# Reordering SyncE's transfers and the last unit's output in a hand-scheduled attention and MLP kernel

## The chip, the cores and the metric

The kernel runs on one core of one Trainium2 chip, as one program in one launch. The metric is the device time of that launch in microseconds (us); less is better. The core has five engines that run side by side and wait for each other through semaphores: TensorE (PE, matrix multiplies), VectorE (DVE), ScalarE (ACT, exponentials and copies), GpSimd (POOL) and SyncE (SP), which here does nothing but issue transfers (DMAs). Each engine executes its own queue strictly in order, so an instruction that waits holds up everything behind it on its engine.

## The reference

All tensors are float32; S is 2048, D is 512, there are 32 heads of 16, and F is 1792.

```python
def _A_ref(x, wqkv, wo):                       # attention
    qkv = (x @ wqkv).reshape(B, S, 3, H, Dh)...
    scores = einsum("bhqd,bhkd->bhqk", q, k) * Dh ** -0.5
    o = einsum("bhqk,bhkd->bhqd", softmax(scores), v)
    return o.transpose(...).reshape(B, S, D) @ wo

def _B_ref(x, w1, b1, w2, b2):                 # MLP
    h = maximum(x @ w1 + b1, 0) ** 2
    return h @ w2 + b2

xn = _layernorm(x)
return x + _A_ref(xn, A_wqkv, A_wo) * _silu(_B_ref(xn, B_w1, B_b1, B_w2, B_b2))
```

## The kernel before

**Units and slots.** The attention is cut into 32 units: unit `u` is four heads (`u // 4`) and 512 query positions (`u % 4`). A unit is worked through in 16 steps of 128 keys, so there are 512 steps, and step `st` is done in a *slot* with the number `st`. A slot holds the four score products of a step (`exp_mm`, one PE product and one exponential on ACT for each head), the product of the exponentials with V two steps back (`pv_step(st - 2)`, PE line L401, into the one bank `po`), row maxima of a unit 24 steps ahead (`max_mm`, DVE line L324), and a piece of dense work (MLP or output projection), which an iterator hands out. PE's order is written by hand; the other four engines get their instructions in the order in which the Python code emits them. `later(n, fn)` emits `fn` at the start of the slot `n` later than now.

**The tail.** From slot 486 on no row maxima are left, and the order of a slot is a plain one of exponentials and the last output projections: `wo_last(c)` takes tiles `k = 16 + 4c + tt` of 128 rows, two slots each. For each tile PE makes three products in two halves into the one bank `pd_t` (L223), DVE multiplies the bank with the gate `g` (L759) and adds the partial sum `s` (L760), and SP stores the rows (L761). The next tile may use the bank only after L759. The operands of tiles 16 to 19 come from one load `oc` (`wo_load(0, [3])`), those of tiles 20 to 23 from another (`wo_load(1, [3])`, L677), which reads what the normalised units 28 and 29 stored in `on_d`. Tiles 24 to 27 use unit 30 directly, and tiles 28 to 31 are done at the very end.

**Three chains that cross SP's queue.**
- *Unit 29's normalisation* (`evac`): after its last `pv_step` the bank is copied (ACT), the sums are gathered (SP, L419), inverted (DVE, L425), stored to `r_d` (SP, L428), loaded back broadcast over the partitions into `hl` (SP, `evac_back`, L433), multiplied and split into a high and a low part (POOL, L439 to L441), and stored to `on_d` (SP, four transfers, L448). Only then can `oc` for tiles 20 to 23 be loaded. `EVAC_LAST` gives the slots, counted from the evacuation, at which these steps are emitted.
- *Unit 31's shift* (`shift`): the row maxima of a unit are transposed, negated and split (DVE, L368 to L371), stored to `sh_d` (SP, L377), and loaded as rows into `qe` (SP, four transfers, L392), where the score products read them. Slot 496 is the first that needs unit 31's.
- *The loads of `g` and `s`* (`wo_ask`, L704 and L710), two tiles ahead, and the load of `q6` (L777), which is read at the end.

**The end** (`unit_final`): after the last `pv_step`, DVE transposes each half of `po` in blocks of 32 (`unit_turn`, L789), inverts the sums that stand in one row of each block (L795), multiplies (L796) and transposes back (L799); ACT makes the high part of `thl` (L849), DVE the low part (L854). PE has meanwhile put twelve products of unit 30's neighbours into four banks (L808) and adds three products for each of the four tiles (L861). Then come a gate (`gate`, DVE, L868) and an addition (L872) for each tile, the first two additions on POOL with their stores on ACT's queue, the last two on DVE with stores on SP.

Of the kernel before, what the change touches and what calls it, by code (L numbers as in the profile page):

```python
# [9 lines left out]
F32 = mybir.dt.float32  # L10
F32R = mybir.dt.float32r
AF = mybir.ActivationFunctionType
ALU = mybir.AluOpType
# [4 lines left out]
P = 128  # L18
S = 2048
D = 512  # L20
H = 32
DH = 16
# [5 lines left out]
NU = NQ * 4  # L28
# [4 lines left out]
NPT = 17  # L33
NVT = 7
EVAC = (1, 6, 7, 9, 11, 14)
EVAC_LAST = (1, 3, 4, 5, 7, 9)
GAPS = (24,)
FIRST = 2
W1_LOADS = (13, 14, 16, 20, 23)
# [15 lines left out]
def kernel(  # L55
# [11 lines left out]
    nc = tc.nc  # L67
    xf = x.rearrange("b s d -> (b s) d")
    of = out.rearrange("b s d -> (b s) d")
# [42 lines left out]
    with ExitStack() as ph:  # L112
# [81 lines left out]
        late = []  # L194
# [4 lines left out]
        def later(n, fn):  # L199
            if n:  # L200
                waiting.append((now[0] + n, fn))
            else:
                fn()
# [124 lines left out]
        def max_end(g):  # L328
            for u in [u for u, n in left.items() if n == 0]:
                del left[u]  # L330
                m4 = m4s[u % 2]
                nc.vector.tensor_reduce(m4[:, :16], mxs[u], axis=AX.X, op=ALU.max)
                mxs[u] = m4
                late.append((g + (8 if u == 3 else 6 if u else 0), u))
            u, s = divmod(g, 16)
            if u >= NU:
                return
            qd, qc = divmod(u, 4)
            if qd == 0:
                if qc == 2 and s % 2 == 0 and s < 12:  # L340
                    load_k(1, s // 2)
                if qc == 3 and 9 <= s < 15:
                    load_k(1, s - 3)
            else:
                if qc == 2 and qd + 1 < NQ and s % 2 == 0:
                    load_k(qd + 1, s // 2)
                if qc == 3 and qd + 1 < NQ and s % 2 == 0 and s < 8:
                    load_k(qd + 1, 8 + s // 2)
            if u == 3 and s == 8:
                for j in range(2):  # L350
                    rows = slice(64 * j + 3 * DH, 64 * j + 4 * DH)
                    nc.sync.dma_start(
                        rot["ka"][3][rows, :].bitcast(F32), rot["ka"][2][rows, :].bitcast(F32)
                    )
            at = (12, 14) if u == 1 else (8, 9)
            if s in at:
                load_q_pair(u, "qe", at.index(s), qes.setdefault(u, []))
            at = (6, 10) if u == 1 else (7, 11)
            if s in at and u + 1 < NU:
                load_q_pair(u + 1, "qm", at.index(s), qms.setdefault(u + 1, []))  # L360
# [5 lines left out]
        def shift(u):  # L366
            tr = sp.tile([P, 32], F32, name="tr", bufs=1)
            nc.vector.transpose(tr, mxs[u])  # L368
            sh = sp.tile([P, 2, 32], F32R, name="sh", bufs=1)
            nc.vector.tensor_scalar(sh[:, 0], tr, -1.0, None, op0=ALU.mult)  # L370
            nc.vector.scalar_tensor_tensor(  # L371
                sh[:, 1], tr, -1.0, sh[:, 0].bitcast(F32),
                op0=ALU.mult, op1=ALU.subtract,
            )

            def keep():
                nc.sync.dma_start(  # L377
                    sh_d[u].rearrange("b c i n -> (b c) i n"), sh.bitcast(F32)
                )

            def back():
                for p in range(2):
                    for i in range(2):
                        shift_rows(u, p, i)

            later(1, keep)
            later(2 if u else 6, back)

        to_block = []

# [234 lines left out]
        tail = {}  # L625
# [118 lines left out]
        def wo_last(c):  # L744
            for tt in range(4):
                k = 16 + 4 * c + tt
                wo_ask(k + 2)
                if k in GAPS:
                    yield None, None
                if c == 2 and tt == 3:  # L750
                    [wo_ask(30), wo_ask(31)]
                if k == 18:
                    wo_load(1, [3])
                t0 = c * 512 + tt * P
                g, s = wos.pop(k)
                ps = pd.tile([P, D], F32, name="pd_t")

                def post():
                    nc.vector.tensor_tensor(g, ps, g, op=ALU.mult)  # L759
                    nc.vector.tensor_tensor(g, g, s, op=ALU.add)  # L760
                    later(2, lambda g=g, t0=t0: nc.sync.dma_start(of[t0 : t0 + P, :], g))  # L761

                done_d[0] = ps
                if c < 2:
                    terms = wo_terms(ps, wos["l", c], tt, [3])
                else:
                    hl, w, ts_ = tail["hl"], tail["w67"], slice(tt * P, (tt + 1) * P)
                    terms = terms3(ps, [(
                        lambda a, q, hl=hl, ts_=ts_: hl[q, a, ts_], lambda b, q, w=w: w[q, b]
                    )])  # L770
                yield from halves(terms, (3,), post, 1)
# [21 lines left out]
        def unit_back(i, rows, sm):  # L793
# [5 lines left out]
            nc.vector.transpose(ot, rows.rearrange("p b r -> p (b r)"))  # L799
            return ot  # L800

        def unit_q6(pss, c, tts):

            def both(a, b, n):
                for h, (ps, tt) in enumerate(zip(pss, tts)):
                    r = slice(64 * h, 64 * h + 64)
                    w = tail["w6"][r, b] if h else wos["w"][r, b, 3]
                    nc.tensor.matmul(  # L808
                        ps, wos["q", c][r, a, tt * P : (tt + 1) * P], w, start=(n == 0), stop=False
                    )  # L810

            return [
                lambda n=n, a=a, b=b: both(a, b, n)
                for n, (a, b) in enumerate(((0, 0), (0, 1), (1, 0)))
            ]
# [23 lines left out]
        def unit_final(po):  # L839
            pss = [pm.tile([P, 512], F32, name="pm_t") for tt in range(3)]  # L840
            pss.append(pd.tile([P, 512], F32, name="pd_t"))
            for step in unit_q6(pss[:2], 3, (0, 1)) + unit_q6(pss[2:], 3, (2, 3)):
                step()
            parts = [wos.pop(28 + tt) for tt in range(4)]
            hls, ots = [], []
            for i in range(2):
                ot = unit_back(i, *unit_turn(po, i))
                hl = tail["p"].tile([P, 2, 256], F32R, name=f"thl{i}")
                nc.scalar.activation(hl[:, 0], ot, AF.Copy)  # L849
                hls.append(hl)  # L850
                ots.append(ot)

            def low(i):
                nc.vector.tensor_tensor(  # L854
                    hls[i][:, 1], ots[i], hls[i][:, 0].bitcast(F32), op=ALU.subtract
                )

            def out(tt, n):
                a, b = ((0, 0), (0, 1), (1, 0))[n]
                t = tt % 2  # L860
                nc.tensor.matmul(  # L861
                    pss[tt], hls[tt // 2][:, a, t * P : (t + 1) * P], tail["w7"][:, b],
                    start=False, stop=(n == 2),
                )

            def gate(tt):
                g = parts[tt][0]
                nc.vector.tensor_tensor(g, pss[tt], g, op=ALU.mult)  # L868

            def add(tt, a, b, eng, queue):  # L870
                g, s = parts[tt]
                eng.tensor_tensor(g[:, a:b], g[:, a:b], s[:, a:b], op=ALU.add)  # L872
                queue.dma_start(of[1536 + tt * P : 1536 + (tt + 1) * P, a:b], g[:, a:b])

            low(0)
            for tt, n in ((0, 0), (0, 1), (1, 0), (1, 1), (0, 2), (1, 2)):
                out(tt, n)
            low(1)
            for tt in (2, 3):
                for n in range(3):  # L880
                    out(tt, n)
            gate(0)
            add(0, 0, D, nc.gpsimd, nc.scalar)
            gate(1)
            add(1, 0, D, nc.gpsimd, nc.scalar)
            gate(2)
            gate(3)
            add(2, 0, D, nc.vector, nc.sync)
            add(3, 0, D, nc.vector, nc.sync)

        ph.enter_context(tc.manual_schedule(engines={mybir.EngineType.PE}))
        qs = ExitStack()
# [520 lines left out]
        def dense():  # L1413
            mp = ExitStack()
            yield from mlp_tasks(mp)
            mp.close()
            early.close()
            wo_pools()
            wo_load(0, [0, 1, 2])
            wo_ask(0)  # L1420
            wo_ask(1)
            for _ in range(2):
                yield [], None
            later(3, wo_small)
            yield from wo_part()
            for c in range(3):
                if c == 0:
                    o3.close()
                    wos["q6"] = right(wstk, "q6p", 1)
                    later(3, lambda: load_q6(3))  # L1430
                yield from wo_last(c)

        odd = itertools.chain((0,) * 4, itertools.cycle((1, 0)))
# [178 lines left out]
```

## Time and profile before

| | us |
|---|---|
| three runs | 1628.72, 1630.25, 1631.37 (median 1630.25) |
| profiled execution, its own time | 1627.99 |
| its span, first to last instruction | 1626.2 |
| PE, DVE, ACT, POOL busy | 1610.3, 1362.1, 1188.9, 520.5 |

The profile is of one execution. Its span is 1.8 us shorter than its own time, and that time is 2.26 us below the median of the three runs. Times in the traces count from the start of the span. A busy PE is not a PE at its peak, because matrix products overlap. The granted clock of PE was 0.999 over the span. `SPq` and `ACTq` rows are transfers being issued: the time in such a row is the issuing, not the transfer. In the timeline a number in brackets behind a row is the idle time before it with what ended it.

### The profile page before, as it was taken

How to read it: one execution, taken by the hardware profiler on the slowest of the kernel's cores; microseconds unless marked ns; L12 is line 12 of the kernel's file. 1: busy time of each engine (PE TensorE's matmuls, PEld its weight loads, DVE VectorE, ACT ScalarE, POOL GpSimd, SP SyncE). 2: the span in 40 equal slices, each digit the busy share in tenths (PEclk: the TensorE clock that was granted, in tenths of full speed). 3: DMA queues.
4: the chain of work that ended last, by engine and by line, in shares of the span. 5: the costliest groups of instructions: out<-in, count | busy, mean ns of one | idle time of the engine just before them, and what ended most of it. 6: DMA issues, size and time to landing. Idle time of an engine off the chain costs nothing.

```text
span 1626.2 us, 36026 instructions
## 1 busy us (share of the span) xinstructions
PE 1610.3 (99%) x13656; PEld 936.1 (58%) x13656; DVE 1362.1 (84%) x2359; ACT 1188.9 (73%) x2349; POOL 520.5 (32%) x547
## 2 busy tenths in 40 slices
PE   8999999999999999999999999999999999999998
PEld 6899665556545654664466456545654565445543
DVE  6486888888888888888888888888888888887744
ACT  7212777777777777877777777777777777777786
POOL 6436667133113310321133112311331133226421
PEclk9999999999999999999999999999999999999999
DMA  8877556434343333434343334423542252247564
GB/s 297 235 236 233 175 162 157 127 96 128 81 103 96 103 88 90 127 87 110 83 119 93 85 87 130 112 68 83 141 112 67 70 155 78 55 126 210 188 179 150
DMA packets 163565, 208.16 MB, mean 128 GB/s; under 512 B 59168, under 2 KB 79136, under 8 KB 161824
## 3 DMA queue, kind: packets, MB, share of 16 engines
q1 hardware_dynamic: 163104, 205.33, 44.6%
q8 instruction: 108, 1.77, 0.5%
q14 instruction: 65, 0.53, 0.1%
q10 hardware_dynamic: 288, 0.52, 0.1%
HBM read 148.64 MB, written 55.56 MB: 126 GB/s over the span
## 4 chain that ended last, share of the span: by engine, by line
PE 98%; DVE 1%; DMA 0%; issue 0%; SPq 0%; DVEq 0%; ACT 0%; ACTq 0%
PE po L401 31%; PE pd_t L255 20%; PE pm_t L317 16%; PE se L1201 14%; PE pd_t L223 7%; PE pm_t L1077 4%; PE pd_t L1077 1%; PE se L1047 1%; PE se L981 1%; PE se L317 1%; PE pm_t L1163 0%; PE pd_t L1047 0%; DVE mx L324 0%; DMA xt<-in_A_x_dram 0%; PE pm_t L1201 0%; PE po L981 0%
## 5 line engine op out<-in xcount | busy, mean ns | idle before, releaser
L324 DVE TENSOR_REDUCE mx<-pm_t 128x1 f32<-128x512 f32 x1927 | 1197.3, 684 | 166.9 <-PE pm_t L317 74.0
L1213 ACT ACTIVATE pt<-se 128x512 f32<-128x512 f32 x1996 | 1035.5, 614 | 252.8 <-PE se L1201 210.4
L317 PE MATMUL pm_t<-ka,qm 64*128 64x512 f32 x1927 | 769.6, 420 | 0.0
L1201 PE MATMUL se<-qe,ka 64*128 64x512 f32 x1996 | 673.0, 396 | 0.3 <-ACT pt L1213 0.3
L401 PE MATMUL po<-pt,v 128*32 128x512 f32 x4096 | 545.3, 604 | 0.2 <-DVE tsm L795 0.2
L317 PEld LDWEIGHTS pm_t<-ka,qm 64*128 64x128 f32 x1927 | 338.3, 184 | 237.0 <-DVE mx L324 225.5
L1201 PEld LDWEIGHTS se<-qe,ka 64*128 64x128 f32 x1996 | 337.2, 184 | 18.1 <-ACT pt L1213 1.7
L255 PEld LDWEIGHTS pd_t<-xc,w1s 64*128 64x128 f32 x2352 | 292.0, 186 | 82.2 <-issue 82.2
L255 PE MATMUL pd_t<-xc,w1s 64*128 64x256 f32 x2352 | 332.2, 288 | 0.0
L255 PE MATMUL pd_t<-w2t,hT 64*128 64x512 f32 x1080 | 300.6, 410 | 0.0
L255 PEld LDWEIGHTS pd_t<-w2t,hT 64*128 64x128 f32 x1080 | 179.0, 184 | 83.2 <-issue 75.5
L555 POOL TENSOR_TENSOR r<-r 128x512 f32<-128x512 f32 x56 | 58.2, 1039 | 370.3 <-ACT r L552 370.3
L401 PEld LDWEIGHTS po<-pt,v 128*32 128x32 f32 x4096 | 81.0, 108 | 159.9 <-issue 136.8
L574 POOL TENSOR_TENSOR u<-u,b_t 128x512 f32<-128x512 f32 x16 | 20.6, 1289 | 320.2 <-ACT u L573 286.3
L324 DVE TENSOR_REDUCE mx<-se 128x1 f32<-128x512 f32 x121 | 77.9, 686 | 26.0 <-PE se L317 26.0
L439 POOL TENSOR_TENSOR ot<-ot,hl 128x512 f32<-128x512 f32 x30 | 38.6, 1286 | 173.9 <-DMA hl<-r_d 132.7
L223 PE MATMUL pd_t<-wot,oc 64*128 64x512 f32 x336 | 90.2, 405 | 0.4 <-issue 0.3
L552 ACT ACTIVATE r<-pd_t,b_t 128x256 f32<-128x256 f32 x112 | 47.0, 470 | 57.0 <-PE pd_t L255 53.8
L223 PEld LDWEIGHTS pd_t<-wot,oc 64*128 64x128 f32 x336 | 58.4, 184 | 46.9 <-ACT pt L1213 12.6
L1077 PE MATMUL pm_t<-xT,wr_t 64*128 64x512 f32 x408 | 73.8, 388 | 0.0
L97 POOL TENSOR_TENSOR hT<-r,hT 128x512 fp32r<-128x512 f32 x56 | 72.3, 1291 | 4.7
L223 PE MATMUL pd_t<-w2t,hT 64*128 64x512 f32 x264 | 68.8, 393 | 0.0
(134 smaller groups left out, 1148.4 us busy)
## 6 DMA issues: line engine op xcount, KB each, us to landing
w1s<-w_d SPq DMA_DIRECT2D x196, 256.0 KB
qm<-q_d SPq DMA_DIRECT2D x384, 32.0 KB
ka<-k_d SPq DMA_DIRECT2D x96, 128.0 KB
qe<-q_d SPq DMA_DIRECT2D x384, 32.0 KB
q_d<-hl SPq DMA_DIRECT2D x16, 512.0 KB
g<-g_d SPq DMA_DIRECT2D x32, 256.0 KB
k_d<-hl SPq DMA_DIRECT2D x15, 512.0 KB
hl<-r_d SPq DMA_DIRECT2D x30, 256.0 KB
```

The source lines that it names most:

```text
L97: (lo or nc.gpsimd).tensor_tensor(dst[1], raw, dst[0].bitcast(F32), op=ALU.subtract)
L223: mm = nc.tensor.matmul(out_, lh(r), rh(r), start=first_ and lane == 0, stop=last_ and lane == 1, skip_group_check=True,)
L255: mm = nc.tensor.matmul(out_, lh(r), rh(r), start=first_ and lane == 0, stop=last_ and lane == 1, skip_group_check=True,)
L317: nc.tensor.matmul(ps, qms[u][p][64 * j : 64 * j + 64, qb * P : (qb + 1) * P], kas[qd, p][64 * j : 64 * j + 64, kc * 512 : (kc + 1) * 512] ...
L324: return nc.vector.tensor_reduce(mxs[u][:, c, kc : kc + 1], ps, axis=AX.X, op=ALU.max)
L401: nc.tensor.matmul(po[32 * j : 32 * j + 32, :], vs[qd][:, (4 * kb + j) * VW : (4 * kb + j) * VW + 32], pts[j], start=(kb == 0), stop=(kb = ...
L439: nc.gpsimd.tensor_tensor(ot, ot, hl[:, 1].bitcast(F32), op=ALU.mult)
L552: nc.scalar.activation(r[:, i], ps[:, i * CW : (i + 1) * CW], AF.Relu, bias=b1_t[:, fo : fo + 1])
L555: nc.gpsimd.tensor_tensor(r, r, r, op=ALU.mult)
L1077: mm = nc.tensor.matmul(out_, lh(r), rh(r), start=first_ and lane == first, stop=last_ and lane != first, skip_group_check=True,)
L1201: nc.tensor.matmul(se, kas[qd, j // 2][b : b + 64, kb * P : (kb + 1) * P], qes[u][j // 2][b : b + 64, :], start=True, stop=True,)
L1213: return nc.scalar.activation(pts[j], se, AF.Exp, scale=0.25)
```

## The change

It has two parts.

In the tail, SP's queue is reordered. Unit 29's load of `hl` is emitted one slot later (`EVAC_LAST`); unit 31's shift is emitted one slot after its maxima instead of six, and the load of its rows four slots after instead of two; the `oc` load of tiles 20 to 23 is asked for by tile 17, three slots later, instead of by tile 18; the `q6` load is emitted ten slots after the start of `wo_last` instead of three.

At the end, `unit_scale` replaces the pair of `unit_back`: it transposes the broadcast inverses instead of the products, and multiplies straight from the bank `po`. The low parts of `thl` move from DVE to POOL. PE takes the products of the second half in the order high, high, then low. Tile 29's addition is done by PE: two products with the identity add `s` and the gated `g` in a bank `se`, and ACT copies it out. POOL adds tiles 28 and 30, DVE tile 31. The stores go to SP, ACT, ACT, SP.

```diff
-EVAC_LAST = (1, 3, 4, 5, 7, 9)
+EVAC_LAST = (1, 3, 4, 6, 7, 9)
...
-                late.append((g + (8 if u == 3 else 6 if u else 0), u))
+                late.append((g + {0: 0, 3: 8, NU - 1: 1}.get(u, 6), u))
...
-            later(2 if u else 6, back)
+            later(4 if u == NU - 1 else 2 if u else 6, back)
...
-                if k == 18:
-                    wo_load(1, [3])
+                if k == 17:
+                    later(3, lambda: wo_load(1, [3]))
...
+        def unit_scale(po, i, rows, sm):
+            ot = tail["p"].tile([P, 256], F32, name=f"tot{i}")
+            nc.vector.reciprocal(sm, rows[:, :, DH])
+            nc.vector.transpose(
+                ot.rearrange("p (b r) -> p b r", r=32), sm[:, :, None].to_broadcast([P, 8, 32])
+            )
+            nc.vector.tensor_tensor(ot, po[:, 256 * i : 256 * i + 256], ot, op=ALU.mult)
+            return ot
...
+            both = pe.tile([P, 512], F32, name="se")
+            nc.tensor.matmul(both, ident, parts[1][1], start=True, stop=False)
...
-                ot = unit_back(i, *unit_turn(po, i))
+                ot = unit_scale(po, i, *unit_turn(po, i))
                 hl = tail["p"].tile([P, 2, 256], F32R, name=f"thl{i}")
                 nc.scalar.activation(hl[:, 0], ot, AF.Copy)
+                nc.gpsimd.tensor_tensor(hl[:, 1], ot, hl[:, 0].bitcast(F32), op=ALU.subtract)
...
-            gate(0)
-            add(0, 0, D, nc.gpsimd, nc.scalar)
-            gate(1)
-            add(1, 0, D, nc.gpsimd, nc.scalar)
-            gate(2)
-            gate(3)
-            add(2, 0, D, nc.vector, nc.sync)
-            add(3, 0, D, nc.vector, nc.sync)
+            for i in range(2):
+                for tt, n in ((0, 0), (0, 1), (1, 0), (1, 1), (0, 2), (1, 2)):
+                    out(2 * i + tt, n)
+            for tt in range(4):
+                gate(tt)
+            nc.tensor.matmul(both, ident, parts[1][0], start=False, stop=True)
+            nc.scalar.activation(parts[1][0], both, AF.Copy)
+            add(0, nc.gpsimd)
+            add(2, nc.gpsimd)
+            add(3, nc.vector)
+            store(0, nc.sync)
+            store(1, nc.scalar)
+            store(2, nc.scalar)
+            store(3, nc.sync)
...
-                    later(3, lambda: load_q6(3))
+                    later(10, lambda: load_q6(3))
```

On SP, the place between the store of unit 29's inverses (`r_d29`) and the `oc` load of tiles 20 to 23 reads as follows before the change. `g` and `s` are the loads for tiles 18, 19 and 20 in that order, and `out_0_dram` is the store of tile 16.

```order
L428 DMA r_d29_126<-sm_22797 128x16
L433 DMA hl_22959<-r_d29_126 128x1x512
L704 DMA g_22965<-g_d_136 128x512
L710 DMA s_22967<-sp_d_133 128x512
L704 DMA g_23014<-g_d_136 128x512
L710 DMA s_23016<-sp_d_133 128x512
L777 DMA q63_23042<-on_d3_132 64x2x512 x2
L761 DMA out_0_dram<-g_22801 128x512
L448 DMA on_d3_132<-hl_22959 16x2x512 x4
L704 DMA g_23068<-g_d_136 128x512
L710 DMA s_23070<-sp_d_133 128x512
L677 DMA oc_23075<-on_d3_132 128x2x512
```

The same place on SP after the change; `sh_d31` and the two `qe` rows are unit 31's shift.

```order
L428 DMA r_d29_126<-sm_22797 128x16
L377 DMA sh_d31_96<-sh_22957 128x64
L704 DMA g_22969<-g_d_136 128x512
L710 DMA s_22971<-sp_d_133 128x512
L433 DMA hl_22997<-r_d29_126 128x1x512
L704 DMA g_23020<-g_d_136 128x512
L710 DMA s_23022<-sp_d_133 128x512
L392 DMA qe2_738<-sh_d31_96 2x16x32 x2
L392 DMA qe3_739<-sh_d31_96 2x16x32 x2
L761 DMA out_0_dram<-g_22801 128x512
L448 DMA on_d3_132<-hl_22997 16x2x512 x4
```

The load of `hl`, which stood directly behind the store of the inverses, now stands behind the shift's store and a pair of loads. The shift's store and loads, which stood behind the `oc` load, stand ahead of it, and the `q6` load has left this place. What follows the last row shown is the same in both: the loads for tile 20, then `oc`.

On DVE, the shift (L368 to L371) follows the last reduction of the maxima (L332) after the change; before it, it stood behind the two tiles 16 and 17. The rows are those of DVE after the change.

```order
L332 TENSOR_REDUCE m_169<-mx 128x16
L368 STREAM_TRANSPOSE tr<-m_169 128x32
L370 TENSOR_SCALAR sh<-tr 128x32
L371 SCALAR_TENSOR_TENSOR sh<-tr,sh 128x32
L1492 TENSOR_SCALAR seen<-pd_t 128x1
L759 TENSOR_TENSOR g<-pd_t,g 128x512
L760 TENSOR_TENSOR g<-g,s 128x512
```

At the end of the program DVE's last rows before the change are these; `tt` and `tot` hold a half of the last unit, `thl` its split parts.

```order
L789 STREAM_TRANSPOSE tt_23635<-po 128x256
L795 RECIPROCAL tsm_23637<-tt_23635 128x8
L796 TENSOR_TENSOR tt_23635<-tt_23635,tsm_23637 128x256
L799 STREAM_TRANSPOSE tot_23638<-tt_23635 128x256
L854 TENSOR_TENSOR thl_23633<-tot_23629,thl_23633 128x256
L854 TENSOR_TENSOR thl_23642<-tot_23638,thl_23642 128x256
L868 TENSOR_TENSOR g<-pm_t,g 128x512 x3
L868 TENSOR_TENSOR g<-pd_t,g 128x512
L872 TENSOR_TENSOR g<-g,ts_22810 128x512
L872 TENSOR_TENSOR g<-g,ts_22891 128x512
```

After the change they are these.

```order
L789 STREAM_TRANSPOSE tt_23638<-po 128x256
L804 RECIPROCAL tsm_23640<-tt_23638 128x8
L805 STREAM_TRANSPOSE tot_23641<-tsm_23640 128x256
L808 TENSOR_TENSOR tot_23641<-po,tot_23641 128x256
L874 TENSOR_TENSOR g<-pm_t,g 128x512 x3
L874 TENSOR_TENSOR g<-pd_t,g 128x512
L878 TENSOR_TENSOR g<-g,ts_22891 128x512
```

The four rows for each half stay four, in another order. The two low parts and one addition have left DVE; the multiplication of a half now reads `po`, and so holds that bank one instruction longer.

More of the change, by code (lines that the diff above doesn't have):

```diff
@@ L844, in unit_final @@
             parts = [wos.pop(28 + tt) for tt in range(4)]
-            hls, ots = [], []
+            both = pe.tile([P, 512], F32, name="se")
+            nc.tensor.matmul(both, ident, parts[1][1], start=True, stop=False)
+            hls = []
             for i in range(2):
-                ot = unit_back(i, *unit_turn(po, i))
+                ot = unit_scale(po, i, *unit_turn(po, i))
                 hl = tail["p"].tile([P, 2, 256], F32R, name=f"thl{i}")
                 nc.scalar.activation(hl[:, 0], ot, AF.Copy)
+                nc.gpsimd.tensor_tensor(hl[:, 1], ot, hl[:, 0].bitcast(F32), op=ALU.subtract)
                 hls.append(hl)
[L851 to L856, printed above, removed]
             def out(tt, n):
@@ L868, in gate, with add, store @@
                 nc.vector.tensor_tensor(g, pss[tt], g, op=ALU.mult)
-            def add(tt, a, b, eng, queue):
+            def add(tt, eng):
                 g, s = parts[tt]
[L872 to L881, printed above, removed]
-            gate(0)
-            add(0, 0, D, nc.gpsimd, nc.scalar)
-            gate(1)
-            add(1, 0, D, nc.gpsimd, nc.scalar)
-            gate(2)
-            gate(3)
-            add(2, 0, D, nc.vector, nc.sync)
-            add(3, 0, D, nc.vector, nc.sync)
+                eng.tensor_tensor(g, g, s, op=ALU.add)
+            def store(tt, queue):
+                queue.dma_start(of[1536 + tt * P : 1536 + (tt + 1) * P, :], parts[tt][0])
+            for i in range(2):
[12 more added lines that the diff above has]
+            store(3, nc.sync)
         ph.enter_context(tc.manual_schedule(engines={mybir.EngineType.PE}))
```

## The prediction

> **What bounds the kernel now.** I read the page first, then the windows of the last 130 us, then the chain of waits there, then the timeline of each engine around the rows that the change moves. The page says that PE is the engine that sets the time.
>
> ```profile
> PE 1610.3 (99%) x13656; PEld 936.1 (58%) x13656; DVE 1362.1 (84%) x2359; ACT 1188.9 (73%) x2349; POOL 520.5 (32%) x547
> PE 98%; DVE 1%; DMA 0%; issue 0%; SPq 0%; DVEq 0%; ACT 0%; ACTq 0%
> ```
>
> The windows show that this changes near the end. Their columns are the busy time of PE, weight loads, DVE, ACT and POOL, then the clock, the share of the DMA engines and GB/s.
>
> ```profile
> core 0: us, PE busy (x) PEld busy (x) DVE busy (x) ACT busy (x) POOL busy (x), PEclk, DMA share, GB/s
> 1500.00:1520.00 20.00, 20.00 (x158) 10.97 (x150) 15.59 (x27) 14.59 (x28) 7.71 (x6) 1.00 0.64 199
> 1580.00:1600.00 20.00, 19.77 (x152) 7.38 (x148) 10.50 (x23) 19.61 (x41) 2.30 (x4) 1.00 0.68 225
> ```
>
> Up to 1560 PE is full and ACT has slack. From there to 1611 ACT is busy 19.61 of 20 us and PE 19.77: both are full, and a stall of either one moves the end by its whole length. Nothing before 1559 is moved by the change. So the question is which transfers PE waits for in the tail, and what the last 12 us are made of. SP's timeline of the tail:
>
> ```profile
> 1553.01 0.32 SPq L428 DMA_DIRECT2D r_d<-sm  x1
> 1557.25 0.55 SPq L433 DMA_DIRECT2D hl<-r_d  x1
> 1557.85 0.47 SPq L704 DMA_DIRECT2D g<-g_d  x1
> 1558.37 0.42 SPq L710 DMA_DIRECT2D s<-sp_d  x1
> ...
> 1567.14 1.73 SPq L448 DMA_DIRECT2D on_d<-hl  x4
> ...
> 1570.75 0.37 SPq L677 DMA_DIRECT2D oc<-on_d  x1
> 1571.22 1.20 SPq L761 DMA_DIRECT2D out_dram<-g  x1
> 1572.47 0.43 SPq L377 DMA_DIRECT2D sh_d<-sh  x1
> 1577.14 2.12 SPq L392 DMA_DIRECT2D qe<-sh_d  x4
> ```
>
> The store of unit 29's inverses is issued at 1553.01, and its load comes back only when that store has landed, at 1557.25. POOL's rows follow it, and then PE's first product of tile 20, the first to read this `oc`:
>
> ```profile
> 1563.44 1.28 POOL L439 TENSOR_TENSOR ot<-ot,hl 128x512 f32<-128x512 f32 x1 [1.52 <-DMA hl<-r_d]
> ...
> 1565.83 1.29 POOL L441 TENSOR_TENSOR hl<-ot,hl 128x512 fp32r<-128x512 f32 x1
> 1575.36 0.69 DVE L759 TENSOR_TENSOR g<-pd_t,g 128x512 f32<-128x512 f32 x1 [2.01 <-PE se L1201]
> 1576.53 0.47 PE L223 MATMUL pd_t<-wot,oc 64*128 64x512 f32 x1 [0.25 <-issue]
> ```
>
> The chain of waits has these two rows (start, length, what), the first for the same moment, the second near the end:
>
> ```profile
> 1576.28 0.25 issue
> ...
> 1621.09 1.34 DVE g L872
> ```
>
> The gate of tile 19 freed the bank at 1575.36 + 0.69 = 1576.05, PE was through with its other work at 1576.28, and yet tile 20 began at 1576.53. The chain has this 0.25 us on the path without a name. I read it as the landing of `oc`, 5.78 us after its issue. So unit 29's chain is already just late: inverses, load of `hl` (1557.25 to 1563.44, 6.19 us), POOL (to 1565.83 + 1.29 = 1567.12, 3.68 us), stores and their landing (to 1570.75, 3.63 us), load of `oc` (5.78 us). There is no slack in it; whatever delays its head moves PE.
>
> **The change, SP's queue.** The head is what the new order delays. SP must now issue the store of unit 31's shift, then `g` and `s` of tile 18, before `hl`. The shift's store waits for DVE, whose rows are:
>
> ```profile
> 1559.20 0.22 DVE L332 TENSOR_REDUCE m<-mx 128x16 f32<-128x64 f32 x1
> 1569.00 0.20 DVE L368 STREAM_TRANSPOSE tr<-m 128x32 f32<-128x32 f32 x1
> ...
> 1569.45 0.19 DVE L371 SCALAR_TENSOR_TENSOR sh<-tr,sh 128x32 fp32r<-128x32 f32 x1
> ```
>
> The maxima are complete at 1559.42. The three shift rows take 1569.64 - 1569.00 = 0.64 us, so `sh` is there at about 1560.1. In SP's queue behind this wait stand the loads for tiles 18 and 19, `hl`, and everything of unit 29. `hl` is issued after 0.43 (the shift's store) + 0.47 + 0.42 and gaps of about 0.05 each, at 1561.5 instead of 1557.25: **+4.25 us**. Tiles 18 and 19 are not hurt: their loads slide by some 3 us and are wanted from 1571 on.
>
> How much of the 4.25 us reaches PE? The rows of the chain keep their lengths (6.19, 3.68, 3.63) if nothing else differs, and `oc` is then issued at about 1575.0. Its landing is the uncertain term. As it was, 5.78 us, PE starts tile 20 at 1576.53 + 4.25 = 1580.8. From below: the last of the `qe` loads, issued at about 1578.7, was used at 1580.67 (row below), which makes 2.0 us for a small load, and 512 KB at the best rate of a window here take 1.7 us more, so 3.7 us, 2.1 us less:
>
> ```profile
> 1581.00:1585.00 4.00, 4.00 (x32) 1.52 (x31) 1.42 (x4) 3.92 (x9) 0.00 (x0) 1.00 1.01 316
> ```
>
> The `q6` load no longer runs ahead of it, which speaks for less; but behind `oc` the stores of tiles 17 and 18 and the loads for tile 21 are now issued without any wait between, and share the DMA engines with it, which speaks for more, some 1 us by an estimate from the same rate (three to four transfers of 256 KB at 0.8 us each, a third of which falls inside). I take the row as it stands, and keep -2.1 and +1.0 for the range. POOL's 3.68 and SP's waits may give back a few tenths; they are inside that range.
>
> Unit 31's own part gains little. PE's rows at the first slot that reads its shift:
>
> ```profile
> 1580.54 0.50 PE L223 MATMUL pd_t<-wot,oc 64*128 64x512 f32 x1
> 1580.67 0.47 PE L1201 MATMUL pm_t<-qe,ka 64*128 64x512 f32 x1
> ```
>
> The two start 0.13 us apart where others start together, because the `qe` loads had ended their issue only at 1577.14 + 2.12 = 1579.26. With the shift stored at 1560.1 they are loaded by about 1567, and this goes: **-0.1 us**. More than that no row of this execution offers.
>
> `q6`, moved behind the store of tile 18 or later, is read from 1614 on: nothing. DVE's shift rows now stand ahead of tile 16's gate and end before its bank is ready: nothing. Each wait of PE behind tile 20 is inherited by the whole rest of the program, since both engines are full.
>
> **The change, the end.** Rows of the last 10 us, and one of the same shape as the low parts on POOL:
>
> ```profile
> 1587.61 0.79 POOL L97 TENSOR_TENSOR hl<-tot,hl 128x256 fp32r<-128x256 f32 x1
> ...
> 1616.16 0.42 ACT L849 ACTIVATE thl<-tot 128x256 fp32r<-128x256 f32 x1 [2.87 <-DVE tot L799]
> 1617.73 0.42 ACT L849 ACTIVATE thl<-tot 128x256 fp32r<-128x256 f32 x1 [1.16 <-DVE tot L799]
> 1618.18 0.43 DVE L854 TENSOR_TENSOR thl<-tot,thl 128x256 fp32r<-128x256 f32 x1 [0.17 <-ACT thl L849]
> 1618.60 1.89 DVE L868 TENSOR_TENSOR g<-pm_t,g 128x512 f32<-128x512 f32 x3
> 1619.33 0.86 PE L861 MATMUL pd_t<-w,thl 128*128 128x512 f32 x3
> 1619.38 2.51 POOL L872 TENSOR_TENSOR g<-g,ts 128x512 f32<-128x512 f32 x2 [29.79 <-DVE g L868]
> 1620.41 0.68 DVE L868 TENSOR_TENSOR g<-pd_t,g 128x512 f32<-128x512 f32 x1
> 1621.01 2.02 DVE L872 TENSOR_TENSOR g<-g,ts 128x512 f32<-128x512 f32 x2
> 1622.46 0.93 SPq L873 DMA_DIRECT2D out_dram<-g  x2
> ```
>
> The high parts come as before (four DVE rows a half, before and after, of the same sizes). The second low part on POOL ends at 1618.2 + 0.79 = 1619.0, later than DVE's 1618.61, but only two products wait for it instead of four, so PE ends at about 1619.75 instead of 1620.19. Gates then end at about 1620.85 instead of 1621.09. One addition is left on DVE. It meets POOL's second addition: POOL's first starts behind the low part at 1619.05, and two take 2.51, so POOL is busy to 1621.6. The second row of the chain above (an addition of 1.34 us that ran against POOL until 1621.89 and ended 0.54 later) says that DVE gets through only when POOL is done, so it ends at 1621.6 + 0.6 = 1622.2 instead of 1623.03: **-0.8 us**. PE's identity products are a form the tail does not show. The nearest row, in the first 60 us, is a full-float32 transpose of a quarter of the width:
>
> ```profile
> L1163 PE MATMUL pm_t<-ident,xn 128*128 128x128 f32 x64 | 11.2, 309 | 6.5 <-ACT xn L1156 6.5
> ```
>
> So one costs between 0.39 (a narrow-mode product of this width takes 0.39 to 0.5 above) and 4 x 0.31 = 1.24 us. I take 0.9. The first runs while PE waits for the high part; the second follows the gates and ends by 1621.0, ACT's copy by 1621.6, and neither is last. [...] Bounds of this part: -1.4 (DVE's addition not held up) to +0.3 (a broadcast transpose at twice 0.45 on both halves).
>
> **The sum** against the profiled execution: +4.25 - 0.1 - 0.8 = +3.35 us, 1631.3 instead of 1627.99. The median of the runs lies 2.26 above that execution, so I forecast 1630.25 + 3.35 = **1633.6 us**, 0.205% slower. A measurement of this kernel can tell about 0.2%, 3.3 us, from no change, and the forecast stands right on that line.
>
> **Rivals.** *`oc` lands quickly.* It gains the 2.1 us of the lower bound, as the traffic ahead of it is gone: +1.2, 1631.5, within 0.2%. For it: 5.78 us is long for 512 KB. Against it: the denser queue behind. [...] *There is slack after all, and it is not slower.* If the 0.25 us at tile 20 were not the load's, and `oc` had landed by 1572.3, the 4.25 us would be absorbed and the gains remain: -0.9 to -1.2, 1629.2. It decides from 1.5 us between issue and landing of `oc`; the shift's store, issued at 1572.47, took until 1577.14, so I hardly believe it. Faster by over 0.2% it would be if the timed runs' 2.26 us above the profiled execution were waits for unit 31's late shift in slot 496, which the new order takes away: -0.9 - 2.3 = -3.2, 1627.0.
>
> **Chances.** The forecast 0.58, of which 0.44 lies beyond 3.3 us and 0.14 short of it (the line runs near its middle, but the denser traffic pulls up); quick `oc` 0.22; late `hl` 0.06; slack 0.08; slack with the shift's waits gone 0.06. So slower by over 0.2%: 0.44 + 0.06 = 0.50; within: 0.14 + 0.22 + 0.08 = 0.44; faster: 0.06. The range takes the forecast with -2.1 - 0.6 - 0.7 (run to run) below and +1.0 + 1.1 + 0.3 above: 1630.2 to 1636.0.
>
> **What would show it.** Right: `hl` issued at about 1561.5, POOL's L439 at about 1567.7, `oc` issued near 1575, a wait of 3 to 5 us on PE at tile 20's first product and on ACT behind it, no gap of 0.13 at slot 496, and the last store 0.8 us sooner after `po`. Wrong: `hl` issued before 1558, or PE passing tile 20 without a wait, or a last store no sooner after `po`.

## The result, and the profile after

| | median us | runs |
|---|---|---|
| before | 1629.70 | 6 (1628.57 to 1631.37) |
| changed | 1636.40 | 6 (1635.03 to 1636.78) |

The ratio is 1.0039, with a 95% interval of 1.0026 to 1.0052; by the medians the changed kernel is 6.7 us slower. The profiled execution took 1636.26 us, its span 1634.4. That is 8.2 us more span than in the profile of before. But the store of unit 29's inverses (`r_d`), ahead of everything that the change moves, already starts 1.50 us later (1554.51 against 1553.01). Two kernels of the experiments below whose code is the same up to that store differ there by 1.76 us (1552.92 and 1554.68), so this is the spread between executions. The change accounts for 8.2 - 1.5 = 6.7 us in the traces, the same as in the times. Times of two traces are compared from here on by their distance from `r_d`.

In the windows, the stretch that was full before is no longer full (columns as in the prediction):

```profile
1580.00:1600.00 20.00, 16.03 (x110) 6.39 (x112) 7.88 (x18) 14.10 (x28) 2.31 (x4) 0.83 0.68 215
```

PE is busy for 16.03 of 20 us where it had 19.77, ACT for 14.10 instead of 19.61, and the clock column says 0.83. SP's timeline shows the head of the delay:

```profile
1554.51 0.32 SPq L428 DMA_DIRECT2D r_d<-sm  x1
1562.35 0.32 SPq L377 DMA_DIRECT2D sh_d<-sh  x1
...
1563.72 0.55 SPq L433 DMA_DIRECT2D hl<-r_d  x1
...
1565.35 2.13 SPq L392 DMA_DIRECT2D qe<-sh_d  x4
...
1573.94 1.74 SPq L448 DMA_DIRECT2D on_d<-hl  x4
...
1577.56 0.37 SPq L677 DMA_DIRECT2D oc<-on_d  x1
```

`hl` is issued 9.21 us after `r_d`; before the change it was 4.24. The engines' timeline shows what follows, POOL's first row for unit 29 and PE's first product of tile 20:

```profile
1570.55 1.28 POOL L439 TENSOR_TENSOR ot<-ot,hl 128x512 f32<-128x512 f32 x1 [7.09 <-DMA hl<-r_d]
...
1583.74 0.76 PE L223 MATMUL pd_t<-wot,oc 64*128 64x512 f32 x1 [5.94 <-DMA oc<-on_d]
```

PE stands idle for 5.94 us, and what ended the wait now has a name, the load of `oc`. The same moment in the chain of waits:

```profile
1577.56 5.83 DMA oc<-on_d
1583.39 0.35 issue
```

The 0.35 us of "issue" behind a landing may be the same kind of piece as the 0.25 that the prediction read as the landing of `oc`. The timeline of DVE and POOL shows why the shift was late even for its new place:

```profile
1560.78 1.28 POOL L737 TENSOR_TENSOR ts<-ts,g 128x512 f32<-128x512 f32 x1 [3.86 <-ACT ts L736]
...
1560.99 0.21 DVE L368 STREAM_TRANSPOSE tr<-m 128x32 f32<-128x32 f32 x1
1561.24 0.86 DVE L370 TENSOR_SCALAR sh<-tr 128x32 fp32r<-128x32 f32 x1
1562.13 0.19 DVE L371 SCALAR_TENSOR_TENSOR sh<-tr,sh 128x32 fp32r<-128x32 f32 x1
```

L370 takes 0.86 us for 32 columns; it ends at 1562.10, just behind POOL's multiplication at 1562.06. Last, the windows behind the wait, cut where the clock changes:

```profile
1576.59:1580.00 3.41, 1.21 (x10) 0.16 (x8) 1.38 (x2) 1.72 (x4) 0.00 (x0) 1.00 0.74 177
1580.00:1583.41 3.41, 0.00 (x0) 0.00 (x0) 0.00 (x0) 0.00 (x0) 0.00 (x0) 0.50 0.91 268
1583.41:1586.83 3.42, 3.09 (x16) 1.46 (x16) 0.16 (x1) 2.25 (x5) 0.00 (x0) 0.50 1.05 406
1586.83:1590.00 3.17, 3.17 (x26) 1.48 (x22) 1.39 (x2) 2.12 (x5) 0.00 (x0) 1.00 1.07 265
```

The granted clock is halved from 1580.00 to 1586.83. In the first half of that PE only waits, which costs nothing. From 1583.74 on it works, for 3.09 us, at half clock. The last part begins where DVE takes up the last unit. Its row in the timeline of before:

```profile
1614.42 0.45 DVE L789 STREAM_TRANSPOSE tt<-po 128x256 f32<-128x256 f32 x1 [3.21 <-PE po L401]
```

and the same row after the change, with the rows that end the program (L878 is the addition of tile 31, formerly L872):

```profile
1622.99 0.45 DVE L789 STREAM_TRANSPOSE tt<-po 128x256 f32<-128x256 f32 x1 [3.21 <-PE po L401]
...
1624.47 1.12 PE L855 MATMUL se<-ts,ident 128*128 128x512 f32 x2
...
1628.31 1.02 PE L888 MATMUL se<-g,ident 128*128 128x512 f32 x2
...
1629.59 1.26 DVE L878 TENSOR_TENSOR g<-g,ts 128x512 f32<-128x512 f32 x1
```

From tile 20's first product to L789 it takes 1622.99 - 1583.74 = 39.25 us, where it took 1614.42 - 1576.53 = 37.89. That is 1.36 us more for the same work, all of it behind the wait. From L789 to the end of the last addition it takes 7.86 us instead of 8.61, 0.75 less, but to the end of the span 1634.4 - 1622.99 = 11.4 instead of 1626.2 - 1614.42 = 11.8, only 0.4 less.

So the time went to three places: tile 20 starts 1583.74 - 1554.51 = 29.23 us after `r_d` instead of 23.52 (+5.71), the stretch behind it is 1.36 longer, and the end is 0.4 shorter. Together that is +6.7 us.

### The profile page after: what moved, and what is told of

It reads as the page before. It is cut to its first block, busy times and chain, and to the rows that moved or that the text cites. A ratio compares the mean times of both kernels' runs of the same rounds, so it can differ in the third digit from the quotient of the medians.

```text
span 1634.4 us, 36038 instructions
## 1 busy us (share of the span) xinstructions
PE 1614.5 (99%) x13660; PEld 943.1 (58%) x13660; DVE 1360.9 (83%) x2356; ACT 1190.5 (73%) x2350; POOL 522.6 (32%) x549
## 4 chain that ended last, share of the span: by engine, by line
PE 98%; DVE 1%; DMA 1%; issue 0%; SPq 0%; ACT 0%; ACTq 0%; DVEq 0%
PE po L401 31%; PE pd_t L255 20%; PE pm_t L317 16%; PE se L1208 13%; PE pd_t L223 7%; PE pm_t L1084 4%; PE pd_t L1084 1%; PE se L1054 1%; PE se L988 1%; PE se L317 1%; DVE mx L324 0%; PE pm_t L1170 0%; DMA oc<-on_d 0%; PE pd_t L1054 0%; DMA xt<-in_A_x_dram 0%; PE pm_t L1208 0%
## 5 line engine op out<-in xcount | busy, mean ns | idle before, releaser
L401 PE MATMUL po<-pt,v 128*32 128x512 f32 x4096 | 545.8, 605 | 0.2 <-DVE tsm L795 0.2
L401 PEld LDWEIGHTS po<-pt,v 128*32 128x32 f32 x4096 | 81.0, 108 | 160.1 <-issue 137.0
```

Of the source, the lines that this page charges most:

```text
L401: nc.tensor.matmul(po[32 * j : 32 * j + 32, :], vs[qd][:, (4 * kb + j) * VW : (4 * kb + j) * VW + 32], pts[j], start=(kb == 0), stop=(kb = ...
```

## The experiments

Theory: SP's wait for unit 31's shift, with `hl` queued behind it, delays `oc` by more than its slack; PE waits, and pays once more because the clock falls. Rivals: the traffic around `oc`'s new place makes it late, or the new end costs the time. The first four kernels were compared with before in one set of runs (before 1629.38 us), the last three in another (before 1629.25).

| kernel | median us | ratio to before, 95% interval |
|---|---|---|
| changed, `hl` one slot sooner | 1628.98 | 0.9996 [0.9987, 1.0005] |
| before, with the new end alone | 1628.74 | 0.9996 [0.9987, 1.0005] |
| before, with SP's new order alone | 1636.30 | 1.0043 [1.0030, 1.0056] |
| before, with `hl` one slot later alone | 1628.52 | 0.9997 [0.9988, 1.0006] |
| changed, PE kept busy in the wait | 1634.18 | 1.0032 [1.0021, 1.0044] |
| changed, shift one slot later | 1629.89 | 1.0006 [0.9997, 1.0015] |
| changed, `hl` in four transfers | 1634.96 | 1.0036 [1.0023, 1.0048] |

### `hl` ahead of the shift again

```diff
-EVAC_LAST = (1, 3, 4, 6, 7, 9)
+EVAC_LAST = (1, 3, 4, 5, 7, 9)
```

> The changed kernel with one number put back: unit 29's load of hl is emitted in the slot it had before, so that it stands on SP directly behind the store of the inverses and ahead of the shift's store and its wait for DVE. Everything else of the change stays. Theory (the wait of SP for unit 31's shift, with hl behind it, holds up unit 29's chain, and the long stall of PE at tile 20 then also costs a spell at half clock): hl is issued within 0.2 us of the landing of the inverses, PE waits under 1 us at tile 20, no spell at half clock, and the kernel is 0.3 to 1.5 us faster than before, 7 to 8 us faster than the changed one. Rival 1 (the loads put close behind oc, and oc's own later place, make it land late): still 3 us or more slower than before. Rival 2 (the new end costs what was measured): still 4 us or more slower than before.

One number of the changed kernel takes the whole loss away, 1628.98 us. By the medians that is 0.4 us faster than before, inside the 0.3 to 1.5 expected, but the interval includes 1. SP's timeline, and PE's two products with V on both sides of tile 20's first half:

```profile
1552.90 0.32 SPq L428 DMA_DIRECT2D r_d<-sm  x1
1557.39 0.55 SPq L433 DMA_DIRECT2D hl<-r_d  x1
...
1569.89 0.37 SPq L677 DMA_DIRECT2D oc<-on_d  x1
...
1575.12 1.06 PE L401 MATMUL po<-pt,v 128*32 128x512 f32 x8
1577.24 1.07 PE L401 MATMUL po<-pt,v 128*32 128x512 f32 x8
```

`hl` is issued 4.49 us after `r_d`, `oc` 16.99 (before: 17.74; changed: 23.05). The two products with V are 2.12 us apart. Before the change they were 2.45 apart (1575.21 and 1577.66) and in the changed kernel 9.02 (1576.73 and 1585.75). So the new place of the `oc` load and the stores behind it are harmless, and the rival of the traffic falls. The 0.33 us by which 2.12 undercuts 2.45 holds the 0.25 that the prediction read as a late `oc`: with `oc` sooner it is gone.

### The new end alone

The diff is the end's half of the change (`unit_scale` and all of `unit_final`), put into the kernel of before; SP's order stays as it was.

> The kernel before with the new end alone; SP's order in the tail is that of before. Theory: 0.4 to 1.1 us faster than before, the last store issued about 0.75 us sooner after the last transposes begin. Rival 1: the same. Rival 2: 4 us or more slower.

The time does not move beyond its interval: 0.9996 [0.9987, 1.0005]. DVE's first and last row of the end in its timeline:

```profile
1614.79 0.45 DVE L789 STREAM_TRANSPOSE tt<-po 128x256 f32<-128x256 f32 x1 [3.21 <-PE po L401]
...
1621.40 1.26 DVE L878 TENSOR_TENSOR g<-g,ts 128x512 f32<-128x512 f32 x1
```

They span 7.87 us, as in the changed kernel (7.86), and the span ends at 1626.2, 11.4 after L789. The end brings some 0.4 us in the traces, which these runs cannot tell from nothing, and it is not where the loss is.

### SP's new order alone

The diff is the other half: the five lines on `EVAC_LAST`, `late`, `later(4 ...)`, `wo_load(1, [3])` and `load_q6`, with the old end.

> The kernel before with the new order on SP alone (with the shift's place on DVE), and the old end. Theory and rival 1: 7 to 8 us slower than before, with a wait of 5 to 6 us of PE at tile 20 and a spell at half clock behind it. Rival 2: within 1 us of before.

The whole loss is here, 1636.30 us. PE's row in the timeline is nearly that of the changed kernel, with a wait of 5.51 us instead of 5.94:

```profile
1583.35 0.76 PE L223 MATMUL pd_t<-wot,oc 64*128 64x512 f32 x1 [5.51 <-DMA oc<-on_d]
```

The spell at half clock is there too, from 1579.73 to 1586.56.

### `hl` one slot later alone

```diff
-EVAC_LAST = (1, 3, 4, 5, 7, 9)
+EVAC_LAST = (1, 3, 4, 6, 7, 9)
```

> The kernel before with unit 29's load of hl emitted one slot later and nothing else: on SP it stands behind the loads for tile 18, but not behind the shift. Theory: those loads wait for nothing and are issued while SP would wait for the inverses to land, so hl is issued within 0.3 us of where it was; the time is within 1 us of before. Rival 1 (a place behind other loads is what costs): hl lands 1 us or more later and the kernel is 1 to 2 us slower.

This is the line whose undoing cured the changed kernel, put into the kernel of before. By itself it costs nothing, 1628.52 us. SP's timeline says why:

```profile
1552.56 0.32 SPq L428 DMA_DIRECT2D r_d<-sm  x1
1552.92 0.43 SPq L704 DMA_DIRECT2D g<-g_d  x1
...
1556.69 0.55 SPq L433 DMA_DIRECT2D hl<-r_d  x1
```

The loads of tile 18 pass ahead of `hl` while it would wait for `r_d` anyway, and `hl` goes out 4.13 us after `r_d`. The slot is harmless; what stands in the queue between `r_d` and `hl`, and what that waits for, is not.

### PE kept busy in the wait

```diff
+                if k == 20:
+                    for _ in range(22):
+                        nc.tensor.matmul(
+                            ps, wos["l", 0][:, 0, 0, :P], wos["w"][:, 0, 3], start=True, stop=True,
+                            skip_group_check=True,
+                        )
```

> The changed kernel, with 22 further TensorE products of 512 columns ahead of tile 20's first product, into the same PSUM bank and overwritten by it: their operands lie ready (tile 16's weights and activations), so they run while the engine would wait for oc. They add work and take no wait away. Theory (the late oc costs twice: about 5.7 us of waiting, and then about 1.4 us because the granted clock falls to 0.5 after 2.2 us of idleness and comes back 3.1 us after the engine starts again): oc lands when it did, tile 20 starts within 0.3 us of where it started in the changed kernel, the granted clock stays at 1.0 from 1577 to 1587 us, the output products of that slot take 1.06 us and not 1.57, and the time is 0.9 to 1.5 us below the changed kernel's: ratio to before 1.0030 to 1.0034 (1634.9 to 1635.5 us beside 1630). Rival (the clock only shows the wait and costs nothing of its own, since ScalarE bounds that stretch): the clock stays up, the time does not move, ratio 1.0039 or more.

PE's timeline has the added products (L765) where the wait was; then a window over the place, and DVE's first row of the end (six lines further down here):

```profile
1576.14 5.28 PE L765 MATMUL pd_t<-wot,oc 128*128 128x512 f32 x22
1582.07 0.47 PE L223 MATMUL pd_t<-wot,oc 64*128 64x512 f32 x1 [0.64 <-DMA oc<-on_d]
...
1620.02 0.45 DVE L795 STREAM_TRANSPOSE tt<-po 128x256 f32<-128x256 f32 x1 [3.21 <-PE po L401]
```

```profile
1577.00:1587.00 10.00, 9.36 (x57) 5.77 (x56) 1.54 (x3) 4.29 (x9) 0.00 (x0) 1.00 0.98 295
```

`oc` is no sooner: `r_d` is at 1552.92 here, so tile 20 starts 29.15 us behind it, against 29.23. But the clock stays at 1.00, and from tile 20 to the end's first row it takes 1620.02 - 1582.07 = 37.95 us: as before the change (37.89), and 1.30 less than in the changed kernel (39.25). In the traces, added work that nobody reads makes the kernel faster. The timed ratio, 1.0032, is where the theory put it, but its interval overlaps that of the changed kernel, so the size of 1.3 us rests on the traces.

### The shift one slot later

```diff
-                late.append((g + {0: 0, 3: 8, NU - 1: 1}.get(u, 6), u))
+                late.append((g + {0: 0, 3: 8, NU - 1: 2}.get(u, 6), u))
```

> The changed kernel with one number altered: unit 31's shift is put two slots and not one behind its last maximum, and the order of SyncE's chains stays as changed. In SyncE's queue the load of hl then stands ahead of the shift's store again. Theory (the harm is only that hl stands behind the wait for the shift): hl is issued within 1 us of the landing of r_d, oc lands before TensorE comes to tile 20, no fall of the clock, ratio 0.9985 to 1.0008, as with hl's slot one sooner. Rival (a later shift makes unit 31's own gates or its first products late, which the sooner shift was to cure): a new wait of 0.3 us or more at unit 31's first slots, ratio over 1.0010.

The loss is gone here too, 1.0006 [0.9997, 1.0015], with the shift's store behind `hl`. But the expectation that `oc` would be there in time was wrong. SP's, POOL's, DVE's and PE's timeline:

```profile
1567.80 1.74 SPq L448 DMA_DIRECT2D on_d<-hl  x4
1569.58 2.11 SPq L392 DMA_DIRECT2D qe<-sh_d  x4
...
1572.74 0.83 SPq L677 DMA_DIRECT2D oc<-on_d  x1
...
1562.32 1.28 POOL L738 TENSOR_TENSOR ts<-ts,xr 128x512 f32<-128x512 f32 x1
...
1562.34 1.29 DVE L370 TENSOR_SCALAR sh<-tr 128x32 fp32r<-128x32 f32 x1
...
1579.29 0.47 PE L223 MATMUL pd_t<-wot,oc 64*128 64x512 f32 x1 [1.32 <-DMA oc<-on_d]
```

The shift's four loads now stand between the stores of `on_d` and `oc`, and issuing them takes SP 2.11 us; `oc` follows `on_d` after 4.94 us instead of 3.61, and PE waits 1.32 us. The clock does not fall for that. And L370 now takes 1.29 us, beside POOL's next instruction: it ends at 1563.63, and POOL's at 1563.60.

### `hl` in four transfers

```diff
-            nc.sync.dma_start(
-                ev["hl"][:, 1].bitcast(F32), r_d[u][:, None, :].to_broadcast([4, 32, 512])
-            )
+            if u == 29:
+                for j in range(4):
+                    nc.sync.dma_start(
+                        ev["hl"][32 * j : 32 * j + 32, 1].bitcast(F32),
+                        r_d[u][j : j + 1, :].to_broadcast([32, 512]),
+                    )
+                return
```

The other units keep the one transfer.

> The changed kernel with unit 29's load of hl written as four transfers of one head each (32 partitions, 64 KB) in place of one of 4 x 32 partitions; the bytes and the place in the queue are the same, SyncE issues three more. In the changed kernel the one load took 6.83 us from its issue to POOL's start. Theory of the stall alone gives no time for this. [...] Rival (the load's 6.8 us are mostly a fixed latency and other loads ahead of it, not its own bytes): hl lands no sooner, three more issues make it 0.5 to 1.4 us later, ratio 1.0039 to 1.0050.

SP's, POOL's and PE's timeline:

```profile
1554.03 0.32 SPq L428 DMA_DIRECT2D r_d<-sm  x1
...
1563.24 1.78 SPq L435 DMA_DIRECT2D hl<-r_d  x4
...
1567.05 1.29 POOL L446 TENSOR_TENSOR ot<-ot,hl 128x512 f32<-128x512 f32 x1 [4.07 <-DMA hl<-r_d]
...
1570.76 2.99 SPq L455 DMA_DIRECT2D on_d<-hl  x4
...
1575.72 0.37 SPq L684 DMA_DIRECT2D oc<-on_d  x1
...
1581.42 0.47 PE L223 MATMUL pd_t<-wot,oc 64*128 64x512 f32 x1 [4.10 <-DMA out_dram<-g]
...
1620.81 0.45 DVE L796 STREAM_TRANSPOSE tt<-po 128x256 f32<-128x256 f32 x1 [3.21 <-PE po L401]
```

The load itself became quicker, against the rival: POOL starts 3.81 us after the first issue instead of 6.83, 3.02 us sooner for the same bytes. Which DMA engines moved what, the run does not show.

The kernel did not follow: 1.0036, beside 1.0039 for the changed kernel. Tile 20 starts 27.39 us behind `r_d`, only 1.84 sooner. Its row puts the end of PE's wait down to the store of an output tile, issued 0.47 us behind `oc`; the product reads `oc` and nothing of that store, so the wait is taken here as one for `oc`, though the row does not name it. The four stores of `on_d` took 2.99 us to issue, against 1.74, so `oc` followed them after 4.96 us instead of 3.62; no row names the cause. And the clock fell all the same: from tile 20 to the end's first row it takes 1620.81 - 1581.42 = 39.39 us, 1.50 more than before the change. The windows show a fall that comes after PE is at work again:

```profile
1575.28:1578.70 3.42, 2.04 (x18) 0.64 (x14) 1.39 (x2) 2.55 (x6) 0.00 (x0) 1.00 0.71 199
1578.70:1582.11 3.41, 0.69 (x6) 0.69 (x8) 0.00 (x0) 0.15 (x1) 0.00 (x0) 1.00 0.96 305
1582.11:1585.53 3.42, 3.42 (x18) 1.00 (x16) 0.16 (x1) 2.41 (x5) 0.00 (x0) 0.50 1.09 394
```

So a wait that is shortened from 5.94 to 4.10 us still pays the whole price of the clock.

## Why the prediction was wrong in its size

**What held.** The bound (PE and ACT both full, no slack in unit 29's chain), the culprit (`hl` behind SP's wait for the shift), the place (PE's wait at tile 20), the inheritance by the rest, and the sign. The kernels with half of the change and with `hl` put back show the culprit, the place and the sign. The rival of slack falls: with `oc` issued 0.75 us sooner (16.99 behind `r_d` instead of 17.74) PE gained only 0.33, so `oc` had been just late. The rival of a quick `oc` falls too: it took 6.18 us from issue to PE, not less than 5.78. The range ended at 1636.0 and the time was 1636.4; the forecast of 3.35 us was half of the 6.7. The terms below make up the rest: 0.72 for the shift's rows, 0.74 for the rest of the chain, 1.36 for the clock, 0.4 for the end and 0.1 for unit 31, together 3.32 us.

**The shift's rows: 0.64 us forecast, 1.33 taken.** The prediction took their lengths from a place where POOL was idle. At the new place POOL runs L737. All three rows took 0.64 us before the change, 0.18 of it L370; beside an instruction of POOL, L370 alone took 0.86 us in the changed kernel and 1.29 with the shift one slot later, and ended 0.04 and 0.03 us behind that instruction. What holds it there, the traces do not show. The prediction had looked for a collision of DVE with POOL at the end only, where it had a row for it. `hl` was issued 4.97 us later, not 4.25.

**The rest of the chain: forecast unchanged, +0.74 taken.** From the issue of `hl` to POOL 6.83 us instead of 6.19, POOL to the stores 3.39 instead of 3.70, the stores to `oc` 3.62 as before (3.61), `oc` to PE 6.18 instead of 5.78. The prediction had the first only as a chance of 0.06 for a late `hl` and as the 1.1 us in its range, and the last in its upper bound (+1.0 for the denser queue), and took zero for both in the sum. No run shows that 1.1: in the runs with two loads ahead of it, `hl` took 4.94 to 6.83 us from issue to POOL, at most 0.64 more than before the change. What lengthened `hl` and `oc` here is not shown: the same load of `hl` took 6.19 us before the change and 5.12 with its slot put back, both times directly behind `r_d`. The two, less the 0.31 that POOL gave back, make 4.97 + 0.74 = 5.71.

**The clock: no term, 1.36 taken.** This is the step that failed in mechanism; the terms above were only mis-sized. The prediction wrote that a stall moves the end by its whole length, and that the rest of the program inherits it. The wait cost more than itself, since PE came back at half clock (the eight products L401 that began at half clock took 1.57 us, the next eight 1.06); the run with added products took 1.30 of it away without bringing `oc` sooner. All nine traces agree: from tile 20's first product to the end's first row it takes 37.86 to 37.95 us in the six in which the clock stays up there, and 39.25 to 39.39 in the three in which it falls. The prediction named 3 to 5 us of idleness as what to look for and had no term for what the clock does then, though the trace of before has such a fall in its windows, behind PE's last product:

```profile
1622.00:1624.00 2.00, 0.00 (x0) 0.00 (x0) 1.03 (x2) 0.00 (x0) 0.00 (x0) 0.61 0.77 285
```

PE had nothing left to do there. The 0.61 is a mean: windows on both sides of 1622.44 read 1.00 and 0.50. The run with four transfers had the fall, and 1.50 us behind it, after a wait of 4.10 us, less than the 4.25 us by which the forecast itself delayed `hl`.

**The end: 0.8 forecast, 0.4 gained.** The compute part came out as worked out: 0.75 us sooner at the last addition. The identity products took 1.12 and 1.02 us for two rows each, inside the bounds of 0.39 and 1.24. The second hid where it was said to. The first ends, by its row, 0.45 us behind the high part that PE was waiting for (1625.59 and 1625.14), and PE's last product of the four tiles came 5.48 us behind L789 instead of the 5.33 worked out; the additions hid that. The prediction's upper bound of +0.3 does not follow from its terms: two times 0.45 on top of -0.8 makes +0.1. But the end of the span came 3.55 us behind the last addition instead of 3.17, and the prediction had let the store follow at its old distance. The four stores stand closer together now; that this is why the last one takes longer was not tested.

**Unit 31's 0.13 us: not the shift.** In the changed kernel the loads of `qe` are issued by 1567.5, and the two products at slot 496 still start 0.12 us apart:

```profile
1589.14 0.50 PE L223 MATMUL pd_t<-wot,oc 64*128 64x512 f32 x1
1589.26 0.47 PE L1208 MATMUL pm_t<-qe,ka 64*128 64x512 f32 x1
```

Nothing was gained there: the 0.13 us had not come from the shift. What makes the 0.12 us stays open.

No version was measurably faster than before: the two with the shortest medians, 1628.52 and 1628.98 us, have intervals that include 1.

## What to carry to other kernels

When a step is put ahead of another in a queue that executes in order, ask first what the moved step waits for: a wait that was harmless at its old place holds up everything behind it at the new one (`hl` went out 9.21 us behind `r_d` with the shift's store ahead of it, 4.49 without), and the length of its producers must be read beside what the other engines do at the new time, not the old. Then price a stall of the matrix engine twice: its length, and the half-clock work behind it (here waits of 4.10 to 5.94 us cost 1.36 to 1.50 us more, and a wait of 1.32 us nothing more). A slot number by itself says nothing; the same slot for `hl` was free in one queue and cost some 7 us in the other (1.0039 against 0.9996).

## What the runs showed of the hardware

In the profile of the changed kernel the granted clock of PE falls at 1580.00, comes back at 1586.83 and falls again at 1634.61, just behind the end of the span. These times are 2 and 14 times 3.41 us apart, as on a fixed grid. The stretches at half clock lasted 6.83 us there (1580.00 to 1586.83) and 3.41 in the run with four transfers (1582.11 to 1585.53).

How busy PE was in the last 3.41 us before such a time fits the changes better than how long it has just been idle. Behind windows of 3.41 us with 0.69 and 1.21 us busy (both above) and with 1.16 (1619.03 to 1622.44, before) the clock fell. Behind one with 2.04 (above) it stayed, and behind one with 3.09 it came back. With the shift one slot later the clock stayed up as well (its mean over the span is 1.000): PE's wait of 1.32 us leaves 2.09 us busy in a window of 3.41 that holds the whole wait. Near 1.5 us the busy time of the profile does not decide: behind 1.52 it fell (1576.32 to 1579.73, SP's new order alone), behind 1.53 it stayed (1627.79 to 1631.20, the end of the changed kernel). So it fell after 2.2 us of idleness in the changed kernel (3.41 - 1.21), and 0.7 us after PE had already resumed in the run with four transfers (1582.11 and 1581.42), and it stayed up through the last 5.1 us of the changed kernel, in which PE did nothing (1629.33 to 1634.4).
